# Group 2 of an attention and feed-forward kernel in seven products, with batch 2's attention weights divided before they are turned

## The chip, the cores and the metric

The kernel runs on one core of a Trainium2 chip. The metric is the time of one execution on the device in microseconds; all times below are in microseconds unless marked ns. TensorE is PE in the profile (its weight loads are PEld), VectorE DVE, ScalarE ACT, GpSimd POOL, SyncE SP.

## What is computed

Attention against pooled keys and values, then a feed-forward layer with the activation h - tanh(h):

```
k_p = k.reshape(B, H, Sp, pool, D).mean(axis=3)      # B=8, H=8, S=576, D=64, pool=8, Sp=72
v_p = v.reshape(B, H, Sp, pool, D).mean(axis=3)
scores = scale * np.matmul(q, k_p.transpose(0, 1, 3, 2))
attn = softmax(scores)                               # over the 72 pooled keys
x = np.matmul(attn, v_p)  -> (B*S, H*D) = (4608, 512)
h = x @ w_in                                         # 512 x 2048
out = (h - np.tanh(h)) @ w_out                       # 2048 x 512
```

## The kernel before, in words

**Groups.** The feed-forward layer runs over nine groups of 512 tokens. Groups 0 to 7 are the first 512 tokens of each batch; group 8 is the eight tails of 64 tokens. While group g goes through the feed-forward layer, the attention of batch g+1 is made between its matmuls, in four units of 128 tokens with all eight heads; in some groups there is a fifth unit, the tails of two batches.

**Feed-forward part of a group.** `h_mms` (L445) makes one hidden block of 128 features for the 512 tokens: four matmuls of 512 columns. There are sixteen, in six PSUM banks. After each pair `h_act` does the tanh on ACT (L458) and the subtraction on DVE (L459), which writes gT. The output comes in one of two forms. *Plain* (groups 0, 1, 2): `o_mms` (L513), four token blocks of sixteen matmuls with 512 columns, so 64, in sixteen units of four (the list UNITS), with block 0 and 2 in bank 4, block 1 and 3 in bank 5; `o_store` (L535) copies each bank to o_h. *Seven products* (groups in SEVEN, from 3 on): Strassen's scheme on 2x2 quarters, 7 x 2 x 8 = 112 matmuls of 256 columns (`product`, L591), with sums of gT quarters on DVE and POOL (L573) and corrections at the end (L611, L618, L624 to L629). The scheme needs four sums of w_out quarters, T1 to T4, which `w_sums` makes on DVE in eight pieces (L556), popped from the list w_ops in the output units of groups 1 and 2, four in each. They lie in buffers k_raw[1], v_raw[1] that batch 1 has left.

**Attention of a unit.** `s_mms` (L311): four matmuls of 144 columns put scores of eight heads in two PSUM banks. `s_shift`: DVE takes the maximum per head (L323) and subtracts it (L326) into SBUF. `s_exp`: one exp of 576 columns on ACT (L362) writes E. `e_turn_dma` (L371): a DMA on SP's queue turns two units' E into ET. `av_mms` (L398): six matmuls multiply ET (stationary) by VB, the pooled values of each 128-row piece with a column of ones per head, so the sums come out beside x. `normalise`: DVE takes the reciprocal of the sums (L419) and multiplies (L420) into x_sb. `x_turn_dma` (L428): a DMA turns two units' x into xT, the moving operand of the next group's hidden blocks. Two helpers used in the first unit of the kernel do the exps otherwise: `s_max` (L335, L338) makes minus the scaled maximum, ng, and `s_exp_heads` (L346) has eight exps of 72 columns read PSUM with ng as bias.

**Data.** Loads of q, k, v come on SP's queue; POOL adds up v (L229 to L235), places it in VB by a masked product (`v_place`, L256), adds up k (L214 to L220). A DMA turns k (L272), and two copies place it in KB (L266), on POOL in plain groups, on ACT at the end of groups in SEVEN. q is cast on ACT (L280) and turned by DMA (L286). 

**Order.** Every engine runs its instructions in the order in which the program issues them; semaphores make one engine wait for another. The order is written by hand: `plan` maps a step (negative: after a hidden block, counted back from the end; from 0: after an output unit or product) to items, where "s" is scores and shift, "e" exp, "t" the turn of E, "a" values and normalisation, "x" the turn of x. PLAN7 is the plan of groups in SEVEN. In those the tail's values are not made in the group itself but carried into the next (`carry`), and q's turn, k's turn and the KB copies stand at fixed steps (`seven_more`).

Of the kernel before, what the change touches and what calls it, by code (L numbers as in the profile page):

```python
# [16 lines left out]
POOL = 8  # L17
# [11 lines left out]
NK = H * G  # L29
# [1 line left out]
D1 = D + 1  # L31
NQ = NHID // 2
HC = DM // 2
SEVEN = (3, 4, 5, 6, 7, 8)
SCALE = 1.0 / (POOL * float(D) ** 0.5)


# [1 line left out]
def kernel(  # L39
# [23 lines left out]
    def two(banks, n):  # L63
        b0, b1 = banks
        return PS[:, b0 : b1 + 1 : b1 - b0, 0:n]
# [60 lines left out]
    def xT_of(g):  # L126
        return xTs[g % 2] if g < B else xTt
# [125 lines left out]

    def v_place(b, vs, eng, t0=0, t1=NT):

        eng.tensor_tensor(  # L256
            out=VB[b % 3][:, t0:t1, :, 0:D],
            in0=vs.to_broadcast([128, t1 - t0, 3, D]),
            in1=mask[:, t0:t1, :, :].to_broadcast([128, t1 - t0, 3, D]),
            op=ALU.mult,  # L260
        )

    def k_place(b, kT, engs):
        kv = kT.rearrange("p (m s g) -> p m s g", m=NHP, s=2)
# [66 lines left out]
    def s_max(banks):  # L331
        sc = two(banks, 4 * G).rearrange("p k (h c) -> p k h c", c=G)
        mx = work.tile([128, 2, 4, 1], FP32, name="mx", tag="mx")
        ng = work.tile([128, H], FP32, name="ng", tag="ng", bufs=4)
        nc.vector.reduce_max(  # L335
            out=mx.rearrange("p k h o -> p k (h o)"), in_=sc, axis=AX.X
        )
        nc.vector.tensor_scalar_mul(ng[:, :], mx.rearrange("p k h o -> p (k h o)"), -SCALE)  # L338
        return ng
# [74 lines left out]
        return work.tile([128, 2, 2, 4, D], BF16, name="x_sb", tag="x_sb", bufs=2)  # L414

    def normalise(banks, x_sb):
        ps = two(banks, 4 * D1).rearrange("p k (h d) -> p k h d", d=D1)
        rden = work.tile([128, 2, 4, 1], FP32, name="rden", tag="rden")
        nc.vector.reciprocal(out=rden[:, :, :, :], in_=ps[:, :, :, D:D1])  # L419
        nc.vector.tensor_tensor(  # L420
            out=x_sb,
            in0=ps[:, :, :, 0:D],
            in1=rden.to_broadcast([128, 2, 4, D]),
            op=ALU.mult,
        )

# [6 lines left out]
    def x_turn_pe(x_sb, g, j, b0, eng):  # L433
        xf = x_sb.rearrange("p a h d -> p (a h d)")
        for fb in range(NFB):
            turn(PS[:, b0, fb * 128 : (fb + 1) * 128], xf[:, fb * 128 : (fb + 1) * 128])
        eng(  # L437
            out=xT_of(g)[:, j, :, :].rearrange("p f c -> p (f c)"),
            in_=PS[:, b0, :],
        )  # L440


    def h_mms(g, i, bank):
# [227 lines left out]
    nc.gpsimd.memset(mask[:, :, :, :], 1.0)  # L671
    for base, sign in ((G, 1), (-1, -1)):
        nc.gpsimd.affine_select(
            out=mask[:, :, :, 0],
# [5 lines left out]
            channel_multiplier=sign,  # L680
        )
    nc.gpsimd.memset(mask[64:128, 4, :, :], 0.0)
    for i in range(3):
        nc.gpsimd.tensor_scalar_mul(VB[i][:, :, :, D:D1], mask[:, :, :, :], float(POOL))
# [3 lines left out]
    nc.gpsimd.memset(k_raw[1][64:128, 4, :], 0.0)  # L688


    def k_turn_pe(b, t0, t1, kps):
# [128 lines left out]
    def load_for(g):  # L820


        r = []
        if g + 2 < B:
            if g in SEVEN:
                r += k_pieces(g + 2) + q_pieces(g + 2)
            else:
                r += (v_pieces(g + 1) if g == 2 else []) + q_pieces(g + 2) + k_pieces(g + 2)
        run(r)

    nc.gpsimd.memset(v_raw[0][64:128, 4, :], 0.0)
# [26 lines left out]
    for u in range(16):  # L858
# [42 lines left out]
    run(stores, 2)  # L901


    PAIRS = ((6, 7), (0, 1), (2, 3))
# [4 lines left out]
    P23, P45, P67 = (2, 3), (4, 5), (6, 7)  # L909
    PLAN7 = {  # L910
        -14: [("s", 0)],
        -11: [("e", 0)],
        -10: [("s", 1)],
        -7: [("e", 1), ("t", 0)],
        -6: [("s", 2)],
        -3: [("e", 2)],
        -1: [("sb", 3, P67)],
        0: [("e", 3), ("t", 1)],
# [4 lines left out]
        9: [("sb", 4, P67)],  # L923
        11: [("e", 4), ("t", 2)],
    }
    late, carry, held = [], [], []

    def tail_values(i):
        av_mms(slot_tl, av_tail(i), P67)
        normalise(P67, x_tl[:, 0, :, :, :])  # L930

    def run_late():
        while late:
            late.pop(0)()

    for g in range(1, NG):
        nb = g + 1 if g + 1 < B else None
# [3 lines left out]
        plan = {}  # L941
        if nb is not None:
            units = [(s_block(nb, j), av_block(nb), slot(4 * nb + j)) for j in range(4)]
            s_pairs, a_pairs = [0, 0, 0, 1, 2], [0, 1, 0, 2, 1]
            plan = {
                -12: [("s", 0)],
                -9: [("e", 0)],
                -8: [("s", 1)],
                -5: [("e", 1), ("t", 0)],
                -3: [("s", 2)],  # L950
                0: [("e", 2)],
                1: [("s", 3)],
                3: [("e", 3), ("t", 1)],
                4: [("a", 0)],
                5: [("a", 1), ("x", 0)],
                9: [("a", 2), ("a", 3), ("x", 1)],
            }
            if g == 1:
                plan[-10], plan[-7], plan[-5] = plan.pop(-12), plan.pop(-9), plan.pop(-8)
                plan[-2], plan[-1] = [("e", 1), ("t", 0)], plan.pop(-3)  # L960
            if tail is not None:
                units.append((s_tail(tail), av_tail(tail), slot_tl))
                plan[3].append(("s", 4))
                plan[4] += [("e", 4), ("t", 2)]
                if g == 1:
                    plan[6], plan[7] = plan[4][:1], plan.pop(5)
                    plan[4] = plan[4][1:]
                    plan[10] = plan.pop(9)
                plan[12] = [("a", 4), ("x", 2)]
# [7 lines left out]
        if nb in (5, 7):  # L977
            tail_cast(tail)
        shs = {}

        def seven_more(u):
            if u == 0:
# [9 lines left out]
        def step(kind, n, bk=None):  # L992
            if kind == "t2":
                e_turn_dma(units[2][2], n, n + 1)
                return
            if kind == "t":
                e_turn_dma(units[2 * n][2], 0, 2 if n < 2 else 1)
                if tail and n == (1 if g in SEVEN else 0):
                    turn_tail(tail)
                return  # L1000
            if kind == "x":
                x_turn_dma(xs[n], *((nb, 2 * n, 2) if n < 2 else (B, tail, 1)))
                return
            s, a, sl = units[n]
            if kind == "s" and bk:
                s_mms(s, bk)
                ng = s_max(bk)
                late.append(lambda: s_exp_heads(bk, ng, sl))
            elif kind in ("s", "sb"):
                bk = bk or PAIRS[s_pairs[n]]  # L1010
                s_mms(s, bk)
                shs[n] = s_shift(bk)
            elif kind == "e":
                s_exp(shs[n], sl)
            else:
                bk = bk or PAIRS[a_pairs[n]]
                av_mms(sl, a, bk)
                normalise(bk, xs[n // 2][:, n % 2, :, :, :])

# [23 lines left out]
        for u in range(14 if g in SEVEN else 0):  # L1043
# [9 lines left out]
                evacuate(n, b, nb is not None)  # L1053
            for it in plan.get(u, ()):
                step(*it)
                run_late()
            if nb is not None and u in (9, 10) and carry:
                carry.pop(0)()
            if more:
# [35 lines left out]
        for u, (tb, qd) in enumerate(() if g in SEVEN else UNITS):  # L1095
            o_mms(tb, qd * 4, qd * 4 + 4, 4 + tb % 2)
            if qd == 3:
                o_store(g, tb, 4 + tb % 2, se)
                if g == 1 or tb > 1:
                    run(stores)  # L1100
            for it in plan.get(u, ()):
                step(*it)
            if u == 0 and more:
                pool_k(nb + 1, nc.gpsimd)
            if more:
                if u == (0 if g == 1 else 3):
                    q_turn_dma(nb + 1)
                if u == 0:
                    run(stores)
                if u == (4 if g == 1 else 9):  # L1110
                    k_turn_dma(nb + 1)
                    k_place_kT(nb + 1, ge)
                if u == 11 and nb % 2 == 0:
                    run(tail_pieces(nb // 2))
                    tail_cast(nb // 2)
# [33 lines left out]
```

## Time and profile before

| what | us |
|---|---|
| three runs | 293.09, 293.10, 294.04 (median 293.1) |
| profiled execution, time | 291.9 |
| profiled execution, span from first to last instruction | 290.2 |

The time of an execution holds 1.7 us beside the span. The profile is one execution; a row of a time line gives start, length, engine, line, operation and tiles, how many were merged, and in brackets how long the engine was idle before and what ended that. A row of the chain of waits gives start, length and what the end of the kernel hung on at that time.

### The profile page before, as it was taken

Reading aid. Unit: us, or ns where it says so; the run is one execution under the profiler, and the core shown is the slowest. Engines: PE = TensorE matmul, PEld = TensorE weight load, DVE = VectorE, ACT = ScalarE, POOL = GpSimd, SP = SyncE. Lnnn points to the kernel's source line nnn. Section 1 sums busy time; section 2 is a strip of 40 time slices with the busy share of each in tenths; the row PEclk is TensorE's granted clock in tenths of the full one; section 3 lists DMA queues with packets and bytes.
Section 4 is the critical chain, followed back from the end, with each engine's and each line's share of the span. In section 5 each row is a group of like instructions: output and inputs, shape, how many; then the busy total and the mean of one; then the engine's idle time right before and its main releaser. Section 6 shows DMA issues by size and latency. Waiting matters only on the chain.

```text
span 290.2 us, 5474 instructions
## 1 busy us (share of the span) xinstructions
PE 279.5 (96%) x2154; PEld 179.4 (62%) x2163; DVE 219.1 (76%) x310; ACT 150.5 (52%) x226; POOL 145.3 (50%) x120
## 2 busy tenths in 40 slices
PE   6699999999999999999999999999999999999994
PEld 2489955444554455448944885488548854874583
DVE  6776876888857995599659975996599757935782
ACT  2686653366416841478366735783576336415630
POOL 7839873149411970882799279917930720010000
PEclk9999999999999999999999999999999999999999
DMA  7999999799989999888899788979622641011005
GB/s 224 231 282 273 206 263 249 149 339 270 219 224 252 328 245 175 291 228 203 166 246 292 205 173 228 304 221 165 201 48 44 95 167 21 1 75 73 0 2 145
DMA packets 84474, 54.56 MB, mean 188 GB/s; under 512 B 59904, under 2 KB 73344, under 8 KB 84448
## 3 DMA queue, kind: packets, MB, share of 16 engines
q1 hardware_dynamic: 77744, 45.17, 61.6%
q0 software_dynamic: 6320, 8.65, 14.2%
q10 hardware_dynamic: 384, 0.39, 0.5%
q8 instruction: 17, 0.28, 0.4%
q14 instruction: 9, 0.07, 0.1%
HBM read 36.70 MB, written 9.44 MB: 159 GB/s over the span
## 4 chain that ended last, share of the span: by engine, by line
PE 85%; DVE 6%; ACT 4%; DMA 2%; issue 1%; SPq 0%; ACTq 0%
PE PS L445 34%; PE PS L591 24%; PE PS L513 14%; PE PS L398 4%; PE PS L465 4%; PE PS L311 3%; DVE gT L459 3%; DMA q_raw<-in_q_dram 2%; PE PS L292 1%; DVE sh L326 1%; DVE mx L323 1%; ACT qT L701 1%; ACT t_sb L458 1%; ACT ET L381 1%; ACT E L362 1%
## 5 line engine op out<-in xcount | busy, mean ns | idle before, releaser
L445 PE MATMUL PS<-xT,w1b 128*128 128x512 bf16 x448 | 100.8, 379 | 0.0
L459 DVE TENSOR_TENSOR gT<-PS,t_sb 128x1024 bf16<-128x1024 f32 x64 | 76.8, 1219 | 28.8 <-ACT t_sb L458 28.8
L458 ACT ACTIVATE t_sb<-PS 128x1024 f32<-128x1024 f32 x64 | 65.6, 1025 | 45.6 <-PE PS L445 43.8
L445 PEld LDWEIGHTS <-w1b 128*128 128x128 bf16 x512 | 49.4, 98 | 55.2
L591 PEld LDWEIGHTS <-gT 128*128 128x128 bf16 x480 | 46.3, 98 | 5.9
L513 PE MATMUL PS<-w2b,gT 128*128 128x512 bf16 x183 | 44.7, 379 | 0.5
L591 PE MATMUL PS<-w2b,gT 128*128 128x256 bf16 x288 | 34.4, 272 | 0.0
L573 POOL TENSOR_TENSOR gT<-gT 128x1024 bf16<-128x1024 bf16 x8 | 16.8, 2120 | 29.1 <-DVE rden L419 29.1
L513 PEld LDWEIGHTS <-gT 128*128 128x128 bf16 x192 | 17.4, 98 | 17.4
L323 DVE TENSOR_REDUCE mx<-PS 128x8 f32<-128x576 f32 x35 | 26.2, 749 | 1.6 <-PE PS L311 1.6
L326 DVE TENSOR_TENSOR sh<-PS,mx 128x576 f32<-128x576 f32 x35 | 26.5, 757 | 1.2
L362 ACT ACTIVATE E<-sh 128x576 bf16<-128x576 f32 x31 | 21.2, 684 | 9.4 <-DVE sh L326 9.3
L420 DVE TENSOR_TENSOR x_sb<-PS,rden 128x512 bf16<-128x512 f32 x32 | 22.1, 692 | 1.1
L229 POOL TENSOR_TENSOR v_raw<-v_raw 128x1280 f32<-128x1280 f32 x6 | 17.4, 2900 | 7.9 <-DMA v_raw<-in_v_dram 7.8
L214 POOL TENSOR_TENSOR k_raw<-k_raw 128x1280 f32<-128x1280 f32 x6 | 17.4, 2903 | 4.0 <-DMA k_raw<-in_k_dram 4.0
L618 DVE TENSOR_TENSOR o_h<-PS,q_raw 128x256 f32<-128x256 f32 x20 | 8.5, 424 | 12.6 <-PE PS L591 11.1
L419 DVE RECIPROCAL rden<-PS 128x8 f32<-128x8 f32 x36 | 7.4, 204 | 14.0 <-PE PS L398 14.0
L625 POOL TENSOR_TENSOR o_h<-o_h,k_raw 128x512 f32<-128x512 f32 x5 | 6.4, 1271 | 21.3 <-DVE o_h L618 21.0
L535 ACT COPY o_h<-PS 128x512 f32<-128x512 f32 x10 | 5.8, 583 | 21.1 <-PE PS L513 21.1
L398 PE MATMUL PS<-VB,ET 128*128 128x130 bf16 (+2 forms) x192 | 16.3, 221 | 0.1
L465 PE MATMUL PS<-xT,w1b 128*128 128x128 bf16 x256 | 15.6, 219 | 0.3 <-ACT xT L437 0.3
L398 PEld LDWEIGHTS <-ET 128*128 128x128 bf16 x192 | 13.5, 98 | 2.9 <-ACT ET L381 0.3
(104 smaller groups left out, 364.0 us busy)
## 6 DMA issues: line engine op xcount, KB each, us to landing
k_raw<-in_k_dram SPq DMA_DIRECT2D x14, 512.0 KB, 6.0
q_raw<-in_q_dram SPq DMA_DIRECT2D x12, 512.0 KB, 6.9
v_raw<-in_v_dram SPq DMA_DIRECT2D x12, 512.0 KB, 4.8
out_dram<-o_h SPq DMA_DIRECT2D x10, 512.0 KB, 3.8
out_dram<-o_h SPq DMA_DIRECT2D x12, 256.0 KB, 3.1
w1b<-in_moe_w_in_dram POOLq DMA_DIRECT2D x4, 512.0 KB, 10.3
q_raw<-in_q_dram POOLq DMA_DIRECT2D x2, 1024.0 KB, 15.4
w2b<-in_moe_w_out_dram POOLq DMA_DIRECT2D x4, 512.0 KB, 11.2
```

The source lines that it names most:

```text
L214: eng.tensor_tensor(out=r[:, :, 0:4, :], in0=r[:, :, 0:4, :], in1=r[:, :, 4:8, :], op=ALU.add)
L323: nc.vector.reduce_max(out=mx.rearrange("p k h o -> p k (h o)"), in_=sc, axis=AX.X)
L326: nc.vector.tensor_tensor(out=sh[:, :, :, :], in0=sc, in1=mx.to_broadcast([128, 2, 4, G]), op=ALU.subtract)
L362: nc.scalar.activation(out=E[:, e, :, :].rearrange("p t c -> p (t c)")[:, 0:NK], in_=sh.rearrange("p k h c -> p (k h c)"), func=ACT.Exp, s ...
L398: nc.tensor.matmul(PS[ps, banks[half], D1 * h : D1 * (h + s1 - s0)], lhsT=ET[:, t, c0 : c0 + (ps.stop - ps.start)], rhs=VB[kb][:, t, s0:s1 ...
L420: nc.vector.tensor_tensor(out=x_sb, in0=ps[:, :, :, 0:D], in1=rden.to_broadcast([128, 2, 4, D]), op=ALU.mult,)
L445: nc.tensor.matmul(PS[:, bank, :].rearrange("p (j c) -> p j c", j=R), lhsT=w1b[:, fb, i * 128 : (i + 1) * 128], rhs=xT_of(g)[:, :, fb, :], ...
L458: nc.scalar.activation(out=t_sb[:, :, :], in_=ps, func=ACT.Tanh)
L459: nc.vector.tensor_sub(out=gT[:, i : i + 2, :], in0=ps, in1=t_sb[:, :, :])
L465: mm = nc.tensor.matmul(PS[:, bank, 128 * n : 128 * n + 128], lhsT=w1b[:, fb, (4 * c + n) * 128 : (4 * c + n + 1) * 128], rhs=xT_of(0)[:, ...
L513: mm = nc.tensor.matmul(PS[:, bank, 0 : c1 - c0], lhsT=gT[:, i, tb * 128 : (tb + 1) * 128], rhs=w2b[:, i, c0:c1], start=(i == 0), stop=(i ...
L591: nc.tensor.matmul(ps, lhsT=A[:, i, 128 * b : 128 * b + 128], rhs=B_[:, i, :], start=(n in "24" and i == 0), stop=(i == NQ - 1), skip_grou ...
```

## The change

- SEVEN starts with 2: group 2's output is made by seven products and follows PLAN7. All eight pieces of the weight sums are popped in group 1.
- The attention of batch 2, made in group 1, follows a plan of its own, PLAN1. Its four units go another way: `w_max` gives ng (as `s_max`); `w_exp` (items "X") runs eight exps of 72 columns from PSUM, each with the sum of its columns as a second output (den); `w_div` (items "z") takes the reciprocal and multiplies, on DVE, so that E holds weights already divided; E is turned by DMA as before; `xt_mms` (items "A") multiplies VB (stationary) by ET of two units (256 columns), eight matmuls a pair, four of 128 rows and four of 64, which gives x in turned form in PSUM; `xt_copy` copies it to xT on ACT, or half on ACT and half on DVE. The x turns by DMA of this batch are gone. The tail unit of group 1 goes the old way.
- To let two heads' values stand side by side for that, the columns of ones in VB move (value 0 has its ones behind it, values 1 and 2 form a pair with ones ahead and behind), `v_place` and the ones take two operations instead of one, `normalise` reads the new layout, and the mask holds 1/8.
- In group 1, o_h of blocks 0 and 1 is copied by DVE, batch 3's v loads are issued after output unit 0 (before: in group 2), q's turn after unit 7 (before: 0), the stores of group 0 after unit 3, the next tail's loads after unit 13 (before: in unit 11 of group 2).

The diff, cut to its core:

```diff
-SEVEN = (3, 4, 5, 6, 7, 8)
+SEVEN = (2, 3, 4, 5, 6, 7, 8)
...
     def v_place(b, vs, eng, t0=0, t1=NT):
-        eng.tensor_tensor(
-            out=VB[b % 3][:, t0:t1, :, 0:D],
-            in0=vs.to_broadcast([128, t1 - t0, 3, D]),
-            in1=mask[:, t0:t1, :, :].to_broadcast([128, t1 - t0, 3, D]),
-            op=ALU.mult,
-        )
+        f = VB[b % 3].rearrange("p t s d -> p t (s d)")[:, t0:t1, :]
+        n = t1 - t0
+        for c, s0, s1 in ((0, 0, 1), (D1 + 1, 1, 3)):
+            eng.tensor_tensor(
...
+    def w_max(banks, n):
+        ng = s_max(banks)
+        den = dens[n]
+        e32 = work.tile([128, 2, 4, G], FP32, name="sh", tag="sh", bufs=4)
+        return ng, den, e32
+
+    def w_exp(banks, w, h):
+        ng, den, e32 = w
+        nc.scalar.activation(
+            out=e32[:, h // 4, h % 4, :],
+            in_=PS[:, banks[h // 4], G * (h % 4) : G * (h % 4) + G],
+            func=ACT.Exp,
+            bias=ng[:, h : h + 1],
+            scale=SCALE,
+            accum_out=den[:, h : h + 1],
+        )
+
+    def w_div(w, sl):
...
+        nc.vector.reciprocal(out=rd.rearrange("p h o -> p (h o)"), in_=den[:, :])
+        nc.vector.tensor_tensor(
...
+            in0=e32.rearrange("p k h c -> p (k h) c"),
+            in1=rd.to_broadcast([128, H, G]),
+            op=ALU.mult,
+        )
+
+    def xt_mms(b, sl, b0):
+        ET = sl[1]
+        f = VB[b % 3].rearrange("p t s d -> p t (s d)")
+        ps = flat(b0, 1024)
+        for m in range(NHP):
+            o = ps[:, 256 * m : 256 * m + 256].rearrange("p (e c) -> p e c", e=2)
+            nc.tensor.matmul(
+                o,
+                lhsT=f[:, m, D1 + 1 : D1 + 1 + 2 * D],
+                rhs=ET[:, :, m, :],
...
+            nc.tensor.matmul(
+                o[64:128, :, :],
+                lhsT=f[:, m + 1, 0:D],
+                rhs=ET[:, :, m + 1, :],
...
+    PLAN1 = {
+        -10: [("S", 0, P67)],
+        -9: [("X", 3)],
+        -7: [("X", 3)],
+        -5: [("X", 2)],
+        -3: [("S", 1, P67), ("z", 0)],
+        -1: [("X", 4)],
+        0: [("X", 4)],
+        2: [("S", 2, P01), ("X", 8), ("z", 1), ("t", 0)],
+        3: [("S", 3, P23), ("X", 4), ("sb", 4, P67)],
+        4: [("X", 4)],
+        5: [("e", 4), ("z", 2)],
+        6: [("z", 3), ("t", 1), ("t", 2)],
+        9: [("A", 0, P67)],
+        13: [("A", 1, P23)],
+        14: [("a", 4, P01), ("x", 2)],
+    }
...
-                o_store(g, tb, 4 + tb % 2, se)
-                if g == 1 or tb > 1:
+                o_store(g, tb, 4 + tb % 2, ve if tb < 2 else se)
+                if tb > 1:
                     run(stores)
...
-            if u in (8, 9, 13, 14):
+            if u in (7, 8, 9, 10, 11, 13, 14, 15):
                 w_ops.pop(0)()
```

More of the change, by code (lines that the diff above doesn't have):

```diff
@@ L670 @@
         nc.vector.memset(t[:, :, 4, 64:128], 0.0)
-    nc.gpsimd.memset(mask[:, :, :, :], 1.0)
+    nc.gpsimd.memset(mask[:, :, :, :], 1.0 / POOL)
     for base, sign in ((G, 1), (-1, -1)):
@@ L682, with ones_place @@
     nc.gpsimd.memset(mask[64:128, 4, :, :], 0.0)
-    for i in range(3):
-        nc.gpsimd.tensor_scalar_mul(VB[i][:, :, :, D:D1], mask[:, :, :, :], float(POOL))
+    def ones_place(i):
+        f = VB[i].rearrange("p t s d -> p t (s d)")
+        for c, s0, s1 in ((D, 0, 2), (3 * D1 - 1, 2, 3)):
+            nc.gpsimd.tensor_scalar_mul(
+                f[:, :, c : c + s1 - s0], mask[:, :, s0:s1, 0], float(POOL)
+            )
+    ones_place(0)
     after(load_rows(v_rows, v_bf[0], 0, 0, 2, nc.gpsimd), k0[0])
@@ L925 @@
     }
-    late, carry, held = [], [], []
+    PLAN1 = {
[15 more added lines that the diff above has]
+    }
+    carry, held = [], []
     def tail_values(i):
@@ L997, in step @@
                 e_turn_dma(units[2 * n][2], 0, 2 if n < 2 else 1)
-                if tail and n == (1 if g in SEVEN else 0):
+                if tail and n == 1:
                     turn_tail(tail)
@@ L1003, in step @@
                 return
+            if kind == "X":
+                for _ in range(n):
+                    exps.pop(0)()
+                return
+            if kind == "A":
+                xt_mms(nb, units[2 * n][2], bk[0])
+                xt_copy(nb, 2 * n, bk[0], (se,) if n == 0 else (se, ve))
+                return
             s, a, sl = units[n]
-            if kind == "s" and bk:
+            if kind == "S":
                 s_mms(s, bk)
[L1007 to L1010, printed above, removed]
+                w = ws[n] = w_max(bk, n)
+                exps.extend(lambda h=h: w_exp(bk, w, h) for h in range(H))
+            elif kind == "z":
+                w_div(ws[n], sl)
+            elif kind == "sb":
                 s_mms(s, bk)
```

104 lines of the change are left out of this document (54 added, 50 removed).

## The prediction

> **What bounds the kernel now.** I read the page first (busy shares, then the chain that ended last), then the busy time of each engine group by group, then the time lines of the groups that the change touches.
>
> ```profile
> span 290.2 us, 5474 instructions
> ...
> PE 279.5 (96%) x2154; PEld 179.4 (62%) x2163; DVE 219.1 (76%) x310; ACT 150.5 (52%) x226; POOL 145.3 (50%) x120
> ...
> PE 85%; DVE 6%; ACT 4%; DMA 2%; issue 1%; SPq 0%; ACTq 0%
> ```
>
> TensorE sets the time: every matmul taken away is a gain, and every wait put in front of TensorE is a loss. Next, the table by stage (each window is one group, from its first hidden-layer matmul to the next group's; columns are length, then busy time and instructions of PE, PEld, DVE, ACT, POOL, then clock, DMA share, GB/s).
>
> ```profile
> 53.80:85.44 31.64, 31.30 (x186) 15.62 (x188) 25.89 (x38) 14.81 (x18) 14.79 (x11) 1.00 0.97 253
> 85.44:116.74 31.30, 31.14 (x187) 15.62 (x189) 23.07 (x32) 15.35 (x19) 13.74 (x9) 1.00 1.00 242
> 116.74:145.20 28.46, 28.46 (x217) 19.65 (x216) 22.32 (x29) 16.92 (x26) 19.97 (x13) 1.00 0.88 223
> 145.20:174.83 29.63, 29.46 (x227) 19.84 (x225) 24.17 (x32) 18.03 (x28) 22.20 (x15) 1.00 0.90 228
> 174.83:204.04 29.21, 29.21 (x229) 20.11 (x228) 23.56 (x32) 17.43 (x28) 21.24 (x14) 1.00 0.91 226
> 204.04:233.00 28.96, 28.96 (x226) 19.82 (x224) 24.17 (x32) 16.32 (x26) 15.32 (x11) 1.00 0.44 95
> ```
>
> Rows one and two are groups 1 and 2 (plain); the other four are groups 3 to 6 (seven products). DVE and DMA are the second limits, so waits can come from them. The prices on TensorE stand in the chain:
>
> ```profile
> 60.01 0.25 PE PS L311 x4
> ...
> 72.58 0.38 PE PS L311 x8
> ...
> 75.65 0.36 PE PS L398 x6
> ...
> 82.26 0.65 PE PS L398 x12
> ...
> 131.71 3.49 PE PS L591 x32
> ...
> 259.94 13.81 PE PS L445 x64
> ...
> L591 PEld LDWEIGHTS <-gT 128*128 128x128 bf16 x480 | 46.3, 98 | 5.9
> ```
>
> A 512-column matmul costs 13.81/64 = 0.216 us, a 256-column one 3.49/32 = 0.109: columns only, for the weight loads (98 ns) are hidden. The change trades 64 of the first (13.81) for 112 of the second (12.21).
>
> **Group 2.** It becomes a group of the seven kind with a tail unit and nothing carried in: that is group 6, 28.96. Gain 31.30 - 28.96 = **2.34**. The tail's values (0.65) are carried into group 3, which becomes a group without tail but with a carry, as group 5 is: 29.21 instead of 28.46, loss **0.75**.
>
> [...]
>
> **Group 4** loses 0.67 today (29.63 against group 6, of the same make). Its first tanh waits behind the copies of KB on ACT, which wait for the kT transpose; DVE, with no slack in these groups, passes the delay on to TensorE.
>
> ```profile
> 146.86 0.89 ACT L266 COPY KB<-kT 64x288 bf16<-64x288 bf16 x2 [2.83 <-DMA kT<-kd]
> 147.77 1.02 ACT L458 ACTIVATE t_sb<-PS 128x1024 f32<-128x1024 f32 x1
> ...
> 176.65 1.02 ACT L458 ACTIVATE t_sb<-PS 128x1024 f32<-128x1024 f32 x1 [0.22 <-PE PS L445]
> ...
> 205.87 1.02 ACT L458 ACTIVATE t_sb<-PS 128x1024 f32<-128x1024 f32 x1 [1.07 <-PE PS L445]
> ...
> 165.24 1.05 PE L591 MATMUL PS<-v_raw,q_raw 128*128 128x256 bf16 x8 [0.17 <-DVE q_raw L573]
> ```
>
> At the start of group 5 the copies were in time with 0.22 to spare, at that of group 6 with 1.07. What differs is TensorE's work behind the last values: group 3 has neither tail nor carry, group 4 a tail (0.38), group 5 a carry (0.65). After the change group 2 ends as group 4 does now and group 3 as group 5: neither is late. Gain **0.67**. Groups 2 to 4 together: 2.34 - 0.75 + 0.67 = **2.26**.
>
> **Group 1, TensorE.** A pair of blocks takes 8 matmuls of 256 columns, 0.87, for two blocks of six, 0.72: +0.15, twice, **+0.30**. I book the 64-row halves at the same price, since columns set it.
>
> **Group 1, ACT.** This is the open cost. One exp of 576 columns becomes eight of 72 that also emit a sum.
>
> ```profile
> 2.68 0.20 ACT L664 ACTIVATE warm<-warm 128x1 f32<-128x1 f32 x1
> ...
> 11.88 1.80 ACT L346 ACTIVATE E<-PS,ng 128x72 bf16<-128x72 f32 x8 [1.06 <-DVE ng L338]
> ...
> 61.16 1.03 ACT L458 ACTIVATE t_sb<-PS 128x1024 f32<-128x1024 f32 x1 [0.90 <-PE PS L445]
> ...
> 66.59 1.02 ACT L458 ACTIVATE t_sb<-PS 128x1024 f32<-128x1024 f32 x1 [0.89 <-PE PS L445]
> 67.51 1.04 ACT L280 CAST q_bf<-q_raw 128x1024 bf16<-128x1024 f32 x1
> 68.44 0.68 ACT L362 ACTIVATE E<-sh 128x576 bf16<-128x576 f32 x1
> ...
> L346 ACT ACTIVATE E<-PS,ng x8: 312/334/364, 11.9 to 13.3; 128x72 bf16<-128x72 f32 x8
> ```
>
> Eight without sums take 1.80, one alone 0.334, so one follows the other by s = (1.80 - 0.334)/7 = 0.21 (overlap 0.12). No row shows the sum. It cannot gain, the exps being issued in any case; if it is free, s = 0.21; if it ends the overlap, 0.334; a whole unoverlapped smallest instruction more is 0.21 + 0.20 = 0.41. I take a smallest instruction that overlaps like the rest: 0.21 + 0.20 - 0.12 = **0.29**. [...]
>
> ```profile
> 11.61 0.17 DVE L338 TENSOR_SCALAR ng<-mx 128x8 f32<-128x8 f32 x1
> ...
> 61.43 0.75 DVE L323 TENSOR_REDUCE mx<-PS 128x8 f32<-128x576 f32 x1
> 62.21 0.76 DVE L326 TENSOR_TENSOR sh<-PS,mx 128x576 f32<-128x576 f32 x1
> 62.89 2.35 DVE L459 TENSOR_TENSOR gT<-PS,t_sb 128x1024 bf16<-128x1024 f32 x2
> ...
> 76.05 0.21 DVE L419 RECIPROCAL rden<-PS 128x8 f32<-128x8 f32 x1 [0.38 <-PE PS L398]
> 76.29 0.69 DVE L420 TENSOR_TENSOR x_sb<-PS,rden 128x512 bf16<-128x512 f32 x1
> ...
> 78.12 0.68 DVE L556 TENSOR_TENSOR k_raw<-w2b 128x1024 bf16<-128x1024 bf16 x1
> ...
> 88.47 1.23 DVE L459 TENSOR_TENSOR gT<-PS,t_sb 128x1024 bf16<-128x1024 f32 x1 [3.39 <-ACT t_sb L458]
> ...
> 68.46 0.41 PE L311 MATMUL PS<-KB,qT 128*128 128x144 bf16 x4 [0.19 <-DVE sh L326]
> ...
> 54.95 1.28 DVE L535 COPY o_h<-PS 128x512 f32<-128x512 f32 x2
> ...
> 67.81 1.80 POOL L256 TENSOR_TENSOR VB<-v_raw,mask 128x960 bf16<-128x960 f32 x1
> ...
> DMA to landing us min/median/max: 4.0/4.0/4.0
> ```
>
> Now the wait that is added. The eight exps read banks 6 and 7 directly, so the next scores for these banks queue on TensorE behind the eighth, and all later matmuls behind them.
> - Scores 0 come at 59.8; DVE is in a subtraction, so mx stands at 61.43 as now and ng at 62.4; first exp 62.50. On ACT follow eight exps with two tanh (0.92 each) among them, plus 0.12 for the last's tail: end 62.50 + 8 x 0.29 + 1.84 + 0.12 = 66.78. TensorE has 14 hidden blocks (12.08) and one unit of scores (0.25) done at 66.13 and, with 0.05 for the hand-over, waits **0.70**.
> - Unit 1: hidden blocks end at 68.81, then (0.25 later) tanh until 69.98, four exps, the second q cast (0.93), four exps: 73.35. The tail's scores for the same banks are due at 72.76: **0.64**. Scores 2 and 3 have banks of their own.
> - DVE copies o_h of block 0 only behind max and shift of the tail: bank 4 is late by **0.13**.
> - Units 2 and 3: exps end at 78.0, DVE divides (reciprocal 0.21, product taken as 0.76) until 79.2; the ET transpose issues then and lands 4.0 later, 83.2; its matmuls are due at 83.45. Hidden, by 0.25 only. The first pair (divided at 74.4, landed 78.4) has 0.7 to spare.
>
> Today's waits here are 31.64 - 31.08 = 0.56 (16 x 0.863 hidden, the same for outputs, 1.38 scores, 2.08 values). So group 1 takes 31.08 + 0.30 + 0.70 + 0.64 + 0.13 = 32.85, loss **1.21**. By s = 0.21 the waits are 0.08, 0.28, 0.06: 31.80, loss 0.16. By 0.334 they are 1.07, 1.05, 0.15 and about 0.25 at the second ET: 33.9, loss 2.3.
>
> **Costed at nothing**, with the cover:
> - DVE, group 1: minus four shifts (3.0) and four normalisations (3.6); plus four ng (0.7), four divisions (3.9), four weight sums (2.7), two copies (1.3), half an x copy (0.6). That is +2.6 on 25.9 busy of 32.9; the end is covered, since a group's first subtraction falls 3.0 after its start (88.47 against 85.44) and DVE idled 3.39 before it.
> - SP: two x transposes go; batch 3's v loads move from group 2 to before ET0, once POOL has placed v at about 70. Issued by 71.6, ahead of ET0 at 74.4. The q transpose moves behind ETl; only group 2's first scores, 12 matmuls in, need it. If the loads run late they eat ET0's 0.7.
> - POOL: each placement of v is split. At worst two whole ones, 3.6 instead of 1.80; kT is then later, but its scores are due only in group 2. In the seven groups POOL is busy 15 to 22 of 29 us.
> - In the first 20 us the placement on DVE is split too: 0 to 0.3, I take 0.
>
> **Sum**: -2.26 + 1.21 = **-1.05**. The profiled execution took 291.9 (span 290.2 and 1.7 around it), so 290.85. The runs have median 293.1, 1.2 above it: **292.1**, 0.35% less.
>
> **Rivals.**
> 1. *Sums are free or nearly* (s up to 0.25): loss in group 1 0.16 to 0.75, time 291.0 to 291.6, faster. For it: eight sumless exps already run at 0.21. Against: the sum needs a write of its own.
> 2. *Sums serialise ACT* (other side). The place is the second ET: at s = 0.41 scores 1 and the tail's wait 1.7 and 1.6, unit 3 is divided at 83, its transpose lands at 87 and TensorE waits another 1.6 at 85.3. Group 1 loses 4.8: 293.1 - 2.3 + 4.8 = 295.6. It passes +0.5% from s about 0.38. For it: 32 exps sit on this path. Against: ACT overlaps all small instructions that the trace shows.
> 3. *A late kT stays*: group 3 starts with ACT behind KB, since the spare is 0.22. Plus 0.7: 292.8.
> 4. *The change doesn't do what it says*: half the columns don't halve a matmul. Above 13.81/112 = 0.123 us each the products gain nothing; with the weight load unhidden (0.109 + 0.098) 112 take 23.2 instead of 12.2: 292.1 + 11.0 = 303.1. Groups 3 to 6 as run speak against it. [...]
>
> **How the numbers follow.** Forecast 0.38 and rival 3 0.08, both within 0.5% (1.5 us, about what a measurement can tell from no change): 0.46. Rival 1: 0.36, faster. Rival 2 0.17 and rival 4 0.01: slower 0.18. The range runs from rival 1's 291.0, less 0.1 for run to run, to 294.4; it leaves out the far half of rival 2, rival 4, and little below.
>
> **What would show it.** In the changed profile: group 2 near 29.0 with 112 matmuls of 256 columns; group 3 near 29.2; group 4 near 29.0 with ACT idle before its first tanh; group 1 near 32.9 with TensorE idle on ACT at scores 1 and at the tail's scores. The exps with sums give s directly. Wrong if group 1 waits at the second ET, if group 2 starts with DVE behind, or if s lies outside 0.25 to 0.334.

## The result and the profile after

| | before | after |
|---|---|---|
| median of 4 runs each | 293.13 | 299.94 (299.77 to 300.87) |
| ratio after/before, 95% interval | | 1.0231 (1.0202 to 1.026) |
| span of the profiled execution | 290.2 | 298.2 |

The change costs 6.8 us, 2.3%; the prediction was 292.1. Lines of the kernel after lie about 75 further down from `h_mms` on: L520 is `h_mms`, L588 `o_mms`, L534 the subtraction, L533 the tanh, L341 ng, L461 the exp with sum, L475 the division, L631 the weight sums, L491 and L499 the 128-row and 64-row matmuls of the turned x.

The table by stage of the kernel after, groups 1 to 6 (columns as in the prediction):

```profile
54.94:92.64 37.70, 33.79 (x178) 15.73 (x181) 32.97 (x39) 22.52 (x78) 22.30 (x16) 1.00 0.83 226
92.64:122.29 29.65, 29.29 (x226) 19.68 (x224) 27.32 (x37) 17.63 (x27) 15.86 (x11) 1.00 0.95 206
122.29:151.68 29.39, 29.39 (x229) 20.17 (x230) 23.30 (x32) 17.43 (x28) 21.08 (x14) 1.00 0.96 224
151.68:181.33 29.65, 28.95 (x224) 19.60 (x223) 24.60 (x33) 17.85 (x28) 22.15 (x15) 1.00 0.96 231
181.33:210.72 29.39, 29.39 (x229) 20.21 (x230) 23.14 (x31) 17.47 (x28) 20.75 (x14) 1.00 0.88 223
210.72:240.64 29.92, 29.12 (x226) 19.74 (x224) 24.17 (x32) 16.25 (x26) 15.49 (x12) 1.00 0.43 92
```

Against the rows of before, the span grows by 1.14 up to the start of group 1 (54.94 for 53.80), by **6.06 in group 1** (37.70 for 31.64), by 0.44 in groups 2 to 6 together (148.00 for 147.56) and by 0.36 from group 7 on: 8.0 in all. Group 2 did get shorter by 1.65, but groups 3 and 6 lost more than that again (1.89).

Where TensorE stood in group 1, from its time line after the change:

```profile
61.23 4.48 PE L520 MATMUL PS<-xT,w1b 128*128 128x512 bf16 x20
66.94 1.89 PE L520 MATMUL PS<-xT,w1b 128*128 128x512 bf16 x8 [1.23 <-DVE gT L534]
...
70.21 0.29 PE L314 MATMUL PS<-KB,qT 128*128 128x144 bf16 x2 [1.26 <-ACT sh L461]
...
76.74 0.41 PE L314 MATMUL PS<-KB,qT 128*128 128x144 bf16 x4 [0.81 <-DVE gT L534]
...
81.43 1.89 PE L588 MATMUL PS<-w2b,gT 128*128 128x512 bf16 x7 [0.34 <-DVE o_h L610]
83.16 0.27 PE L491 MATMUL PS<-ET,VB 128*128 128x256 bf16 x1
83.36 0.30 PE L499 MATMUL PS<-ET,VB 128*64 128x256 bf16 x1
...
84.92 3.63 PE L588 MATMUL PS<-w2b,gT 128*128 128x512 bf16 x16
```

There are four waits, three of them for DVE. Counted from start to start they are larger: the row gives the 20 matmuls from 61.23 a length of 4.48, at 0.216 each they are done after 4.32, at 65.55, and the next starts at 66.94, so 1.39. The four are 1.39, 1.41 (scores 1), 1.07 (scores 3 and the tail's), 0.52 (bank 4): 4.39, where 1.47 was predicted. And the eight matmuls of the turned x go from 83.16 to 84.92: 1.76, 0.22 each, not 0.109.

What DVE did at these times, and POOL beside it:

```profile
63.35 2.41 DVE L341 TENSOR_SCALAR ng<-mx 128x8 f32<-128x8 f32 x1
65.68 1.21 DVE L534 TENSOR_TENSOR gT<-PS,t_sb 128x1024 bf16<-128x1024 f32 x1
...
73.48 2.07 DVE L475 TENSOR_TENSOR E<-sh,rd 128x576 bf16<-128x576 f32 x1
...
77.70 0.76 DVE L475 TENSOR_TENSOR E<-sh,rd 128x576 bf16<-128x576 f32 x1
...
84.16 0.68 DVE L631 TENSOR_TENSOR k_raw<-w2b 128x1024 bf16<-128x1024 bf16 x1
...
86.42 3.37 DVE L631 TENSOR_TENSOR v_raw<-w2b,k_raw 128x1024 bf16<-128x1024 bf16 x1
```

```profile
62.85 2.89 POOL L229 TENSOR_TENSOR v_raw<-v_raw 128x1280 f32<-128x1280 f32 x1 [3.70 <-DMA v_raw<-in_v_dram]
...
73.39 1.54 POOL L217 TENSOR_TENSOR k_raw<-k_raw 128x640 f32<-128x640 f32 x1
...
86.04 3.21 POOL L229 TENSOR_TENSOR v_raw<-v_raw 128x1280 f32<-128x1280 f32 x1
```

Read the two together by their ends. ng, eight numbers a lane, took 2.41 instead of 0.17 and ended at 65.76, when POOL's addition ended (65.74). The first division took 2.07 and ended 0.6 after POOL's addition at 74.93; the same division at 77.70, with POOL idle, took 0.76. The fourth weight sum took 3.37 and ended 0.5 after POOL's addition (89.25). The subtraction at 65.68, which reads PSUM, took its usual 1.21 beside POOL. So these three instructions of DVE, which read and write SBUF alone, stood until POOL's addition beside them ended, or 0.5 to 0.6 longer. POOL lost too: its two copies of KB at 84.45, beside three of the weight sums (0.68, 0.79, 0.91), took 1.50, and 0.90 in the kernel before (81.02), where what DVE did beside them reads PSUM.

### The profile page after: what moved, and what is told of

Its sections match the earlier page's. It is cut to its first block, busy times and chain, and to the rows that moved or that the text cites. A ratio compares the mean times of both kernels' runs of the same rounds, so it can differ in the third digit from the quotient of the medians.

```text
span 298.2 us, 5645 instructions
## 1 busy us (share of the span) xinstructions
PE 281.1 (94%) x2197; PEld 183.8 (62%) x2203; DVE 232.6 (78%) x321; ACT 160.8 (54%) x295; POOL 156.6 (53%) x133
## 4 chain that ended last, share of the span: by engine, by line
PE 71%; DVE 15%; DMA 6%; ACT 5%; issue 2%; ACTq 0%; DVEq 0%
PE PS L520 30%; PE PS L666 24%; PE PS L588 5%; DVE gT L534 4%; PE PS L540 4%; PE PS L401 4%; DMA xT<-x_sb 3%; PE PS L314 2%; DMA ET<-E 2%; DVE mx L326 1%; DMA k_raw<-in_k_dram 1%; ACT t_sb L533 1%; DVE sh L329 1%; DVE ng L341 1%; PE PS L295 1%
## 5 line engine op out<-in xcount | busy, mean ns | idle before, releaser
L520 PE MATMUL PS<-xT,w1b 128*128 128x512 bf16 x448 | 101.0, 379 | 2.7 <-DVE gT L534 1.2
L534 DVE TENSOR_TENSOR gT<-PS,t_sb 128x1024 bf16<-128x1024 f32 x64 | 76.7, 1218 | 25.6 <-ACT t_sb L533 25.6
L533 ACT ACTIVATE t_sb<-PS 128x1024 f32<-128x1024 f32 x64 | 65.7, 1026 | 45.8 <-PE PS L520 44.4
L520 PEld LDWEIGHTS <-w1b 128*128 128x128 bf16 x512 | 49.2, 98 | 58.6 <-issue 2.4
L666 PE MATMUL PS<-w2b,gT 128*128 128x256 bf16 x336 | 40.1, 273 | 0.0
L648 POOL TENSOR_TENSOR gT<-gT 128x1024 bf16<-128x1024 bf16 x10 | 21.0, 2121 | 35.9 <-DVE rden L423 29.9
L588 PE MATMUL PS<-w2b,gT 128*128 128x512 bf16 x122 | 29.9, 379 | 0.8 <-DVE o_h L610 0.3
L326 DVE TENSOR_REDUCE mx<-PS 128x8 f32<-128x576 f32 x31 | 23.2, 749 | 2.0 <-PE PS L314 2.0
L329 DVE TENSOR_TENSOR sh<-PS,mx 128x576 f32<-128x576 f32 x31 | 23.5, 757 | 1.1
L427 DVE TENSOR_TENSOR x_sb<-PS,rden 128x512 bf16<-128x512 f32 x28 | 19.4, 692 | 1.2 <-DVE rden L423 0.2
L588 PEld LDWEIGHTS <-gT 128*128 128x128 bf16 x128 | 11.6, 98 | 12.3 <-issue 0.6
L314 PEld LDWEIGHTS <-qT 128*128 128x128 bf16 x128 | 10.1, 98 | 10.2 <-issue 3.3
L314 PE MATMUL PS<-KB,qT 128*128 128x144 bf16 x128 | 13.6, 226 | 2.6 <-ACT sh L461 1.3
L401 PE MATMUL PS<-VB,ET 128*128 128x130 bf16 x168 | 14.6, 221 | 0.9 <-DMA ET<-E 0.8
L686 ACT COPY o_h<-PS 128x256 f32<-128x256 f32 x20 | 7.5, 373 | 14.8 <-PE PS L666 14.8
```

Of the source, the lines that this page charges most:

```text
L314: nc.tensor.matmul(PS[ps, banks[m // 2], KP * (m % 2) : KP * (m % 2) + KP], lhsT=qT[:, m, :], rhs=KB[kb][:, m, :], start=True, stop=True,)
L326: nc.vector.reduce_max(out=mx.rearrange("p k h o -> p k (h o)"), in_=sc, axis=AX.X)
L329: nc.vector.tensor_tensor(out=sh[:, :, :, :], in0=sc, in1=mx.to_broadcast([128, 2, 4, G]), op=ALU.subtract)
L401: nc.tensor.matmul(PS[ps, banks[half], D1 * h : D1 * (h + s1 - s0)], lhsT=ET[:, t, c0 : c0 + (ps.stop - ps.start)], rhs=VB[kb][:, t, s0:s1 ...
L427: nc.vector.tensor_tensor(out=x_sb.rearrange("p k (m h) d -> p k m h d", h=2), in0=ps[:, :, :, 1 : 2 * D1 - 1].rearrange("p k m (h d) -> p ...
L520: nc.tensor.matmul(PS[:, bank, :].rearrange("p (j c) -> p j c", j=R), lhsT=w1b[:, fb, i * 128 : (i + 1) * 128], rhs=xT_of(g)[:, :, fb, :], ...
```

## The experiments

All twelve, with the length of group 1 and of groups 2 to 6 from each one's profile (a single execution has no interval):

| run | ratio to before (95%) | group 1 | groups 2 to 6 |
|---|---|---|---|
| the change | 1.0231 (1.0202 to 1.026) | 37.70 | 148.00 |
| e1 small operands in PSUM | 1.0232 (1.0202 to 1.0263) | 36.81 | 146.71 |
| e2 turned x by size | 1.0272 (1.0228 to 1.0316) | 36.63 | 149.45 |
| e3 no sums | 1.0282 (1.0256 to 1.0307) | 37.72 | 147.82 |
| e4 e1 + e2 + later POOL | 1.0193 (1.0152 to 1.0234) | 35.45 | 147.16 |
| e5 as e1, one bank | 1.0172 (1.0152 to 1.0193) | 35.66 | 147.70 |
| e6 as e4, one bank | 1.0153 (1.0129 to 1.0176) | 34.32 | 148.02 |
| e7 seven products alone | 0.9994 (0.9975 to 1.0013) | 31.63 | 148.49 |
| e8 full rows | one execution, 301.41 | 35.50 | 149.80 |
| e9 as e6, unit 1 in SBUF | 1.0141 (1.0112 to 1.0169) | 33.50 | 147.79 |
| e10 as e7, v loads at 0 | 1.0178 (1.0154 to 1.0202) | 38.02 | 146.63 |
| e11 as e7, v loads at 5 | 1.018 (1.0138 to 1.0221) | 35.89 | 148.29 |
| e12 later POOL alone | one execution, 300.66 | 38.06 | 147.68 |

Theory A: DVE instructions standing behind POOL cause the waits of group 1. Theory B: alternating tile widths make the turned x slow. The main rival: the exps with sums on ACT cause the loss, and DVE is only late with them.

**e12, POOL moved, DVE untouched.**

```diff
-        if nb is not None:
+        if nb is not None and g > 1:
             pool_v(nb, nc.gpsimd)
...
                 w = ws[n] = w_max(bk, n)
+                if n == 0:
+                    after([pool_v(nb, nc.gpsimd)], ngs[0])
```

> The changed kernel, with no instruction of DVE touched: POOL's first addition of batch 2's v is held until ng of unit 0 is done, some 0.8 later than it started. Theory A: ng of unit 0 takes 0.17 instead of 2.41 and the wait of TensorE at the hidden block (1.23) goes; but the later POOL work moves with it, the first division now meets the long addition of k and stands for about 2.7, and scores 3 wait 2 to 2.5 for the subtraction behind it instead of 0.81. Group 1 37.0 to 37.5. Rival (ng is long for a reason of its own): 2.4 as before.

DVE and POOL of e12:

```profile
64.07 0.17 DVE L345 TENSOR_SCALAR ng<-mx 128x8 f32<-128x8 f32 x1
...
72.15 3.30 DVE L480 TENSOR_TENSOR E<-sh,rd 128x576 bf16<-128x576 f32 x1
```

```profile
64.38 2.90 POOL L229 TENSOR_TENSOR v_raw<-v_raw 128x1280 f32<-128x1280 f32 x1 [4.87 <-DVE ng L345]
...
71.94 2.89 POOL L214 TENSOR_TENSOR k_raw<-k_raw 128x1280 f32<-128x1280 f32 x1
```

The same ng takes 0.17, and the division, which now begins 0.2 after POOL's long addition of k, takes 3.30 and ends 0.6 behind it. Scores 3 wait 2.24 for the subtraction behind that division. The stall goes where POOL's work goes: theory A holds. Group 1 came out at 38.06, 0.6 above the expectation; 1.7 of that is a lower clock behind the wait (0.53, last section), without which it would be 36.4, below the expectation.

What the rows of the two runs show side by side: beside POOL's additions the divisions (2.07, and 3.30 in e12) and the weight sum (3.37), which have both inputs in SBUF, and ng (2.41), which goes from SBUF to SBUF, stand; the subtraction, with one of two inputs in PSUM, does not (1.21). Whether one operand in PSUM is enough for ng and the division too is what e1 tries.

**e1, e5, e9: DVE's operands moved, POOL untouched.** The maxima, and the reciprocals for the division, lie in unused columns of the score banks.

```diff
+        mx = PS[:, banks[1], 288:296]            # e1: two(banks, 512)[:, :, 288:292]
...
-        rd = work.tile([128, H, 1], FP32, name="rd", tag="rd")
+        rd = PS[:, banks[1], 296:304]            # e1: two banks; e9: SBUF for unit 1
```

> The changed kernel, with the maxima and the reciprocals of batch 2's four units kept in unused columns of their score banks in PSUM instead of SBUF, so that ng and the division read at most one operand from SBUF; POOL's work stays where it is. Theory A (DVE instructions that read and write only SBUF stand still while POOL works): ng of unit 0 takes 0.2 instead of 2.41 and the division of unit 0 about 0.8 instead of 2.07, beside the same POOL additions; the first exp comes 2.2 earlier, the waits of TensorE at the hidden block (1.23) and at scores 3 (0.81) go, those that the prediction booked (0.70, 0.64, 0.13) stand in their place, group 1 takes 34.7 instead of 37.70, and the kernel is 3.0 faster than the changed one, about 296.9. Rival (the exps with sums on ACT set the waits, and DVE is only late by them): ng gets short but group 1 stays above 37.

> As the first experiment, but maxima and reciprocals lie side by side in one bank, behind the scores. In the first, their two-bank access spanned the scores between them, and the program waited for it where nothing was shared: exps of unit 1 behind the first division, the tail's scores 2.76 behind the second. Without these waits theory A has its full effect: ng and divisions short, waits of TensorE in group 1 about 0.4 at scores 1, 0.65 at the tail's scores, 0.1 at bank 4; group 1 takes 34.4 instead of 37.70, the kernel is 3.0 to 3.3 faster than the changed one, 296.2 to 296.9. Rival (the standing DVE instructions do not set group 1): a new wait of the same size appears elsewhere and group 1 stays above 36.

In e1, ng took 0.17 and the division 0.75 beside POOL's unchanged additions, and the wait at the hidden block was gone, but the time was not better:

```profile
63.07 0.17 DVE L458 TENSOR_SCALAR ng<-PS 128x8 f32<-128x8 f32 x1
70.96 0.75 DVE L479 TENSOR_TENSOR E<-sh,PS 128x576 bf16<-128x576 f32 x1
...
62.50 2.90 POOL L229 TENSOR_TENSOR v_raw<-v_raw 128x1280 f32<-128x1280 f32 x1 [3.68 <-DMA v_raw<-in_v_dram]
70.07 2.90 POOL L214 TENSOR_TENSOR k_raw<-k_raw 128x1280 f32<-128x1280 f32 x1
...
76.41 0.45 PE L314 MATMUL PS<-KB,tl_T 128*64 128x144 bf16 x8 [2.76 <-DVE E L479]
```

The last line's wait is the edit's own: the tail's scores wait for the second division, whose reciprocals lie in the two banks of these scores. So e1 is no test of the size. In e5, with the reciprocals in one of the two banks, two of the tail's eight matmuls went ahead and the other six still waited 1.38 for the division, and group 1 fell by 2.04; the expectation of 34.4 was missed, mainly by that wait. e9 takes it away, with the other two mends in place.

**e2 and e8: the turned x.**

```diff
-        for m in range(NHP):      # 128 rows of m, 64 rows of m, ...
+        for r in range(2):        # e2: first all of 128 rows, then all of 64
+            for m in range(NHP):
...
-                lhsT=f[:, m + 1, 0:D],            # 64 rows
+                lhsT=f[:, m + 1, 0 : 2 * D],      # e8: 128 rows
```

> The changed kernel, with the eight matmuls of the turned x in another order: the four of 128 rows first, then the four of 64 rows. Theory B (each change between a 128-column and a 64-column stationary tile keeps the weight load from being hidden): two changes a pair instead of eight, the eight take about 1.0 instead of 1.76, the kernel is 1.5 faster than the changed one, about 298.4. Rival (64-row tiles, or these operands, are slow by themselves): four or all eight stay at 0.22 and the gain is 0 to 0.2.

> The changed kernel with the 64-row matmuls of the turned x made 128 rows (their stationary operand is 128 columns wide, so half of what they add is wrong data), in the order of the change, each still adding onto the result just written. Theory B (alternating tile widths): all eight at 0.11, 0.87 a pair, group 1 shorter by 1.4 to 1.8. Rival (adding at once onto the result just written is slow): they stay at 0.22.

TensorE in e8:

```profile
83.79 0.27 PE L491 MATMUL PS<-ET,VB 128*128 128x256 bf16 x1
83.90 0.27 PE L499 MATMUL PS<-ET,VB 128*128 128x256 bf16 x1
...
84.66 3.62 PE L588 MATMUL PS<-w2b,gT 128*128 128x512 bf16 x16
```

Eight in 0.87, 0.109 each, with each adding onto the result just written: that is not what costs. In e2 the eight took 1.08 (83.00 to 84.08): 0.87 and 0.1 for each of two changes of width. So a change of width costs about 0.1, as theory B says. Why is seen in the weight loads (PEld) of the 64-row tile, first in the kernel after, then in e8:

```profile
83.36 0.11 PEld L499 LDWEIGHTS <-VB 128*64 128x64 bf16 x1 [0.32 <-issue]
...
83.79 0.10 PEld L499 LDWEIGHTS <-VB 128*128 128x128 bf16 x1
```

In e8 the load begins together with the matmul before its own (83.79); in the kernel after it begins 0.20 behind the start of that matmul (83.16), at the time of its own (83.36), and is not hidden. Neither run got faster, though: group 1 shrank by 1.07 (e2) and 2.20 (e8), and group 2 grew by 1.28 and 1.79. Some 0.4 of the 2.20 is luck of timing: ng began later and stood only 2.05. TensorE reached the next group earlier than DVE's half of the copy of x, which sat behind the stalled weight sums; in e8 it waited 0.96 for it. A gain on TensorE was given back because theory A's stall still stood there.

**e3, the rival.**

```diff
-            accum_out=den[:, h : h + 1],
```

> The changed kernel without the sums that the exps of batch 2 emit (the division is by ones, so batch 2's weights are not normalised). Theory A: exps follow one another at 0.21 instead of 0.295, which shortens the wait at scores 1 by 0.7 and little else; ng and the divisions stay long (2.4, 2.1); 0.7 to 1.3 faster than the changed kernel, 298.6 to 299.2. Rival (the sums on ACT are the cause of the loss): 4 or more faster, below 296.

```profile
66.67 1.89 PE L519 MATMUL PS<-xT,w1b 128*128 128x512 bf16 x8 [1.21 <-DVE gT L533]
...
76.45 0.41 PE L314 MATMUL PS<-KB,qT 128*128 128x144 bf16 x4 [1.52 <-DVE gT L533]
```

The exps did follow one another at 0.21 and scores 1 waited 0.53 instead of 1.26, but DVE reached its division no earlier against POOL, and scores 3 waited 1.52 instead of 0.81. Group 1: 37.72. Even theory A's 0.7 did not show, because the freed time was spent waiting at POOL's next instruction. So the sums are not the cause. The eight shorter exps in place of one stay in every run; what they can cost is bounded by the waits left in e9.

**e4, e6, e9: everything mended.** Besides the above, POOL's first addition of batch 3's v is held until the last weight sum:

```diff
+        if b == 3:
+            after([first], last_w[0])
```

> Maxima and reciprocals in PSUM, the matmuls of the turned x in order of their size, and POOL's addition of batch 3's v held until the last weight sum. Theories A and B together: 3.0 + 1.5 + 0.3 (weight sums at 0.7 each, group 2 starts with DVE less far behind) = 4.8 faster than the changed kernel, 295.1, so still above the kernel before; group 1 about 33.0. If the costs overlap, the gain is less than the sum of the single ones.

> The three mends together, with the one-bank form: maxima and reciprocals in one bank of PSUM, the turned x's matmuls in order of size, POOL's addition of batch 3's v behind the last weight sum. Group 1 about 33.0, group 2 29.5, the kernel 294.3 to 295.0, still slower than before by 1 to 2, because groups 2 to 6 together take no less than before.

> The three mends with one difference: the reciprocal of unit 1 lies in SBUF again, because in one bank with the tail's scores the program still made those wait for the second division (1.38). Theory A and B: the tail's scores wait for the exps alone, about 0.5; the second division stands until POOL's running addition ends, which nothing of TensorE needs at once. Group 1 33.2 to 33.6 instead of 37.70 (with the turned x at 1.08 a pair and the prediction's waits), groups 2 to 6 147.5 to 148, the kernel 295.5 to 296.5. Rival: the waits move once more and group 1 stays above 34.3.

e4 and e6 carry the waits that e1 and e5 brought in, and both missed what was expected: group 1 took 35.45 and 34.32 for 33.0, the kernel 298.11 and 297.63 us. With the hold all weight sums took 0.68 to 0.91. e9 is the clean one: its stage row, and TensorE's waits there.

```profile
54.90:88.40 33.50, 32.68 (x180) 15.80 (x181) 27.89 (x44) 22.33 (x78) 16.74 (x13) 1.00 0.95 254
```

```profile
67.92 0.28 PE L316 MATMUL PS<-KB,qT 128*128 128x144 bf16 x2 [0.40 <-ACT sh L467]
...
74.47 0.44 PE L316 MATMUL PS<-KB,tl_T 128*64 128x144 bf16 x6 [0.34 <-ACT sh L467]
...
74.84 5.59 PE L589 MATMUL PS<-w2b,gT 128*128 128x512 bf16 x24
80.27 1.16 PE L500 MATMUL PS<-ET,VB 128*128 128x256 bf16 x8
```

Group 1 takes 33.50, as expected, 4.20 less than after the change. Counted from start to start its waits are 0.56, 0.74 and 0.25: the last does not stand in brackets, but 24 matmuls from 74.84 need 5.18 and the next starts only at 80.27. That is 1.55 instead of 4.39, and the two pairs of the turned x, 1.09 each instead of 1.76, take 1.34 less: 4.18 of the 4.20. The kernel is still 1.4% slower than before.

**e7, e10, e11: the seven products alone**, on the kernel before.

```diff
-SEVEN = (3, 4, 5, 6, 7, 8)
+SEVEN = (2, 3, 4, 5, 6, 7, 8)
...
-            if u in (8, 9, 13, 14):
+            if u in (7, 8, 9, 10, 11, 13, 14, 15):
...
+                if u == 0:               # e10; e11: u == 5
+                    run(v_next)          # and POOL held as in e9
```

> The kernel before with one part of the change alone: group 2 in seven products, its eight weight sums all in group 1 (twelve more cover slots are not needed: DVE has them beside the output units), attention of batch 2 as before. The prediction's own sum for this part says 2.26 faster, 290.9. The changed kernel's trace says less: group 2 takes 29.65 and not 28.96, group 3 29.23, groups 4 and 6 29.8 and 29.9, so groups 2 to 6 together take 147.8 against 147.4 before; by that the part alone gives nothing: 292.6 to 293.5.

> Group 2 in seven products alone, on the kernel before, once more, with what held it up taken away: batch 3's v loads issued after output unit 0 of group 1 instead of after unit 13 (in the run without this, POOL added v until 102.9 and k until 110.8, so DVE's sums of gT stood at 1.63 and 2.44 instead of 0.69 and 1.22 and TensorE waited in group 2), and POOL's first addition of it behind the last weight sum. Group 2 about 29.5 instead of 31.59, group 1 31.6 to 32.2: 1.3 to 2 faster than before, about 291.5. Rival (DMA is full in group 1, 0.97 of the time): the loads delay the turns of E, k and x there, group 1 takes 32.5 or more and nothing is gained.

> The same with the v loads after output unit 5, behind the second turn of E. If the loads collide with the first turns, this is better than after unit 0; if they collide with the turns of k and x, worse: 291.0 to 293.

e7 is the one part alone and gives nothing, 0.9994. Group 2 took 31.59. Two things come late there, because v is loaded late. POOL's additions of v and k run on into the group, and DVE's sums of gT stand beside them:

```profile
101.79 1.63 DVE L573 TENSOR_TENSOR q_raw<-gT 128x1024 bf16<-128x1024 bf16 x1
...
106.93 2.44 DVE L573 TENSOR_TENSOR S<-gT,q_raw 128x2048 bf16<-128x2048 bf16 x1
```

They take 0.69 and 1.22 elsewhere. That was taken for the cause when e10 was planned, but no row shows TensorE waiting for these sums. Its waits are for ACT's copies, 0.8 and 0.4, and for a turn of E, 1.1 (0.8 in e10). The chain that ended last leads from that turn back to the load of q, issued behind the late loads of v and k:

```profile
92.91 9.94 DMA q_raw<-in_q_dram
...
106.17 0.60 PE L591 MATMUL PS<-v_raw,q_raw 128*128 128x256 bf16 x4 [0.63 <-ACT q_raw L606]
```

q landed at 102.85, ACT began to cast it at 102.95, and the tanh, the copies and E queued behind the casts on ACT. Loading v earlier (e10) mends group 2 by either account, 29.75, and breaks group 1, where the second turn of E lies behind the loads on SP's queue:

```profile
83.19 1.49 PE L400 MATMUL PS<-VB,ET 128*128 128x130 bf16 x12 [3.52 <-DMA ET<-E]
```

The turn took 6.4 to land instead of 3.6 in e7. That is e10's rival. Group 1 took 38.02, 6.4 more than in e7: 3.7 of wait, and 2.7 because the clock was at 0.50 to 0.54 in the 5 to 6 us behind it. In e11 the wait moved to the turn of x at the end of group 1:

```profile
89.42 4.35 PE L447 MATMUL PS<-xT,w1b 128*128 128x512 bf16 x12 [4.09 <-DMA xT<-x_sb]
```

From start to start it is 4.26, the whole of what group 1 lost on e7 (35.89 for 31.63). The clock fell here too: the 12 matmuls took 4.19 instead of 2.59, and without that group 2, 31.51, would have been 29.9. Both runs missed their expectations (297.70 and 297.85 us for at most 293). So group 2 got 1.55 shorter than before with v loaded early (e10), not the 2.34 booked, and the old attention of group 1 left no free stretch of DMA for the loads in the two places tried (DMA share 0.99 in e10 and 1.03 in e11 over group 1). No version tried beats the kernel before.

## Why the prediction was wrong

1. **DVE in group 1, costed at nothing: "That is +2.6 on 25.9 busy of 32.9; the end is covered".** This step failed. It counted DVE's busy time and never asked what POOL does beside it; that busy time came out at 32.97 and not 28.5. Before, the weight sums took 0.68 to 0.69 where POOL was idle, and ng 0.17 at 11.61, as POOL's casts of q ended (11.62); the change put them beside POOL's additions. Waits 4.39 instead of 1.47; 1.55 with the stalls removed and POOL's work for batch 2 in place (e9). Price 2.8 to 2.9.
2. **"I book the 64-row halves at the same price, since columns set it."** This failed too: 0.22 each while the widths alternate, 0.109 when they don't (e8). Price 1.8. Steps 1 and 2 are 4.7 of the 4.85 by which group 1 exceeds its forecast of 32.85.
3. **Exps with sums, s = 0.29: right.** The trace shows the sum as an instruction of its own behind each exp, overlapping with the next:

```profile
77.65 0.32 ACT L461 ACTIVATE sh<-PS,ng 128x72 f32<-128x72 f32 x1 [0.80 <-DVE rd L474]
77.87 0.19 ACT L461 ACTIVATION_READ_ACCUMULATOR sh<-PS,ng 128x1 f32 x1
77.97 0.31 ACT L461 ACTIVATE sh<-PS,ng 128x72 f32<-128x72 f32 x1
```

   Sixteen from 77.65 to 82.41 give 0.2975. The waits worked out from it, 0.70 at scores 1, 0.64 at the tail's scores and 0.13 at bank 4, came as 0.56, 0.74 and 0.25 in e9, where no stall hid them: 1.55 for 1.47. Rival 2 (ACT serialised) did not occur.
4. **Groups 2 to 4, "2.34 - 0.75 + 0.67 = 2.26".** Group 2 took 29.65 and not 28.96, group 3 29.39 (forecast 29.21, right), group 4 29.65 and not 28.96. The mechanism named for group 4 was right: its first tanh no longer waits for kT, ACT idled 1.08 before it for TensorE. What is late in its place is the second turn of x, for which the prediction had no term: it landed at 122.24 and 181.29, and TensorE stood 0.52 and 0.86 for it at the end of groups 2 and 4. The model was group 6, which ran with DMA busy 0.44 of its time; groups 2 and 4 ran with 0.95 and 0.96. That this is what delays the turn is not shown. Group 6, which the change does not touch, lost 0.96 to a turn of E that took 5.13. Predicted gain 2.26, measured loss 0.44.
5. **"In the first 20 us ... 0 to 0.3, I take 0."** It was 1.14. The delay is 0.27 by group 0's first hidden block (18.04 for 17.77), where ng, beside POOL's casts of q, took 0.57 instead of 0.17; it grows by 0.32, to 0.59, up to the scores of a later unit (39.93 for 39.34), which was not followed up, and by 0.55 at the end of group 0, where the second turn of x took 3.58 instead of 2.74 to land and did so at 54.81, 0.13 before TensorE goes on (the row of that start names DVE's addition of k, which ended at 54.94).
6. Right: both turns of E landed in time (81.9 and 87.13, matmuls at 83.16 and 88.38), and a 256-column product costs 0.109. The sign that was named, "group 2 starts with DVE behind", appeared (first subtraction 3.36 after the start), and cost nothing: in e9 it came at 3.04 and group 2 was as long.

## What to carry to other kernels

Before a DVE instruction moves or is added, look at what POOL does at the new place. DVE's busy time was no measure here where DVE read and wrote SBUF alone beside POOL (ng took 2.41 for 0.17, a division 2.07 for 0.76), and the stall of one small instruction held what stood behind it in DVE's order (the subtraction behind ng, and TensorE with it for 1.39). Moving one operand to PSUM (e1: ng 0.17, the division 0.75), or POOL's addition behind DVE's weight sums (e4 and e9: at most 0.91 for 3.37), removed it here; but check that the new operand's place does not bring in an order of its own, as in e1 (a wait of 2.76). Keep matmuls of one tile width together, since a change of width cost about 0.1 here (e2), and judge a form of a stage by the loads, turns and carries that come with it: seven products alone were worth nothing here (e7, 0.9994).

## What the hardware showed unexpectedly

**The clock after a wait.** In e12 TensorE waited 2.24, and the next 24 output matmuls took 6.88 instead of 5.18. The stretch behind the wait, with the granted clock third from the end of the row, and the matmuls on TensorE's time line:

```profile
77.60:81.00 3.40, 3.40 (x10) 1.23 (x9) 3.30 (x7) 2.42 (x17) 0.86 (x1) 0.53 0.10 20
```

```profile
77.36 7.04 PE L593 MATMUL PS<-w2b,gT 128*128 128x512 bf16 x24
84.24 0.27 PE L496 MATMUL PS<-ET,VB 128*128 128x256 bf16 x1
```

So a clock of 0.53 for 3.4, a loss of 1.7 beside the wait. The clock fell behind the wait of 3.52 in e10, to 0.50 to 0.54 for 5 to 6 us, and behind that of 4.09 in e11 (0.95 over the whole of group 2); in e4 a wait of 2.75 left it at 1.00. So a wait of 2.24 was enough once, in e12, and a longer one was not, in e4. What decides was not tried.

**Turns by DMA and the queue q8.** The same quiet turn of E in group 6, by the DMA view around it, after and before:

```profile
q8 instruction: 1, 0.02, 1.1%
ET<-E SPq DMA_TRANSPOSE x1, 5.1
```

```profile
ET<-E SPq DMA_TRANSPOSE x1, 3.4
```

After, one packet of queue q8, which the view names instruction, moved during the turn, and none before; the turn took 5.13 after and 3.45 before. The quiet turn of E ahead of it, with no packet in either profile, took 3.41 in both, and the turn of the tail's q behind it took 4.05 beside the packet after and 2.62 before, where it had none. Not every turn goes this way: in the kernel before, a turn of x at 226.26 took 4.23 beside a packet, where the one behind it took 2.73 without, but one at 142.00 took 2.82 beside a packet, where the one at 171.57 took 2.77 without. So the two go together for some of these turns; that the packet is the cause was not tested.
